# Attention and gated projections on one core: the opening's loads, buffers and casts put in another order

## The chip, the core and the metric

The kernel runs on one core of one Trainium2 chip. The metric is the device time of one execution in microseconds (us). Each execution also records the span of the core and the mean clock that was granted to TensorE, as a share of full speed.

## The reference, cut to what matters

Four batches, 8 heads, 768 positions, head size 64. Blocks of 32 positions attend to their neighbours, to the first and last block and to three drawn blocks. The result is normalised per row and goes through a gated projection of 512 to 1536 and back.

```python
scores = scale * np.matmul(q, k.transpose(0, 1, 3, 2))
scores = np.where(mask, scores, -1e9)              # block mask, 24 x 24 blocks
attn = softmax(scores)
x = np.matmul(attn, v)                             # -> (3072, 512), heads side by side
xn = x / np.sqrt(np.mean(x * x, -1) + 1e-6) * rms_g
g, val = xn @ w_gate, xn @ w_val                   # 512 x 1536 each
out = (g * sigmoid(g) * val) @ w_out               # 1536 x 512
```

## The kernel before

Everything is fed to TensorE. Keys and queries of a pair of heads are cast to bf16 (`aug`), transposed (`XA`), multiplied to scores, exponentiated by ScalarE into a probability buffer (`pt`), and multiplied with the cast values (`vaug`). The mask is part of the product: 24 extra columns of `aug` carry it. For batch 0 the transposes of keys and queries are done by TensorE; for later batches they are DMA transposes (`XA<-aug`), issued on SyncE. The normalised rows (`xq`) must be transposed too (`xn`): for the first NPET units by TensorE, later by a DMA transpose (`xn<-xq`), also issued on SyncE. A unit is a set of query rows: units 0 to 2 are 128 rows each, unit 3 is 384 rows, all of batch 0; units 4 to 9 are 384 rows each of batches 1 to 3. A small scheduler in the program sorts all operations by modelled times at build time; each engine then runs its list in order.

```python
# loads of batch 0; pairs of heads g = 0..3; i = 0 keys, 1 queries, 2 values; 384 KB a keys or values tile
load0(0, 0, slice(0, 1)); load0(0, 0, slice(1, 2))
load0(0, 1, x=slice(0, D)); load0(0, 1, x=slice(D, HD))
load0(1, 0); load0(0, 2); load0(1, 1)              # all on SyncE's queue
# ... later, by the scheduler:
for g, i in ((2, 0), (2, 1), (1, 2), (3, 0), (3, 1), (2, 2), (3, 2)): ...
# the mask columns of both aug buffers, by ScalarE
for t in aug:
    nc.scalar.copy(out=t[:, 1, :, :, D:KQ], in_=qm.unsqueeze(1).to_broadcast([P, 2, NC, NB]))
# zeros behind the mask columns, wanted before batch 1's DMA transposes
def zero_pad():
    for t in aug:
        nc.gpsimd.memset(t[:, :, :, :, KQ:P], 0.0)
# probability buffers, transposed-row buffers, units whose rows TensorE transposes
NPT, NXN, NHP, NPET = 3, 3, 2, 4
# rows of unit u, transposed by the DMA when u >= NPET
op(("cp", u), {"DMA": 1.8}, [("xq", u, t) for t in range(nt)], (-2, u), lambda e, p, u=u: xt(u), ...)
```

The softmax here doesn't subtract the row's maximum and nothing guards it: scores larger than these inputs give would overflow.

Of the kernel before, what the change touches and what calls it, by code (L numbers as in the profile page):

```python
# [9 lines left out]
FP32 = mybir.dt.float32  # L10
# [3 lines left out]
ALU = mybir.AluOpType  # L14
# [3 lines left out]
def kernel(  # L18
# [27 lines left out]
    AHEAD, HURRY, HURU = 0.8, ("av", "xo", "sq", "rsq", "xq", "tr", "cp"), 0  # L46
    NSTARV = 3
    AH = {"uu": 0.3, "hp": 0.3}
# [41 lines left out]
    A = [raw.tile([P, 3, 2, NC * D], FP32, name="qkv", tag="qkv") for g in range(3)]  # L90
    def load0(g, i, e=slice(0, 2), x=None):
        x = x or slice(0, HD if i == 1 else NC * D)
        nc.sync.dma_start(
            out=A[g][:, i, e, x], in_=(kv, qv, vv)[i][0, :, 2 * g:2 * g + 2][:, e, x])

    load0(0, 0, slice(0, 1))
    load0(0, 0, slice(1, 2))
    load0(0, 1, x=slice(0, D))
    load0(0, 1, x=slice(D, HD))
    load0(1, 0)  # L100
    load0(0, 2)
    load0(1, 1)
# [84 lines left out]

    for t in aug:
        nc.scalar.copy(out=t[:, 1, :, :, D:KQ], in_=qm.unsqueeze(1).to_broadcast([P, 2, NC, NB]))  # L189

# [38 lines left out]
    def gate_pool(g):  # L229
        nc.gpsimd.tensor_copy(out=scf, in_=A[g][:, 1, 0, 0:1])  # L230

# [14 lines left out]

    def zero_pad():
        for t in aug:
            nc.gpsimd.memset(t[:, :, :, :, KQ:P], 0.0)

# [29 lines left out]
    def exp(u, pr, g):  # L280
        b, c0, nt = UNITS[u]
        kt, w = KT[nt], nt * P
        if (u, pr) not in pts:
            if nt == 1:
                t_ = work.tile([P, 2, NC, 2, w], BF16, name="pt", tag="pt", bufs=NPT)
                pts[u, pr // 2 * 2], pts[u, pr // 2 * 2 + 1] = t_[:, 0], t_[:, 1]
            else:
                pts[u, pr] = work.tile([P, NC, 2, w], BF16, name="pt", tag="pt", bufs=NPT)
        s_ = tiles.pop(("s", u, pr, g))
        nc.scalar.activation(  # L290
            out=pts[u, pr][:, g * kt:(g + 1) * kt].rearrange("p j e w -> p e j w"),
            in_=s_[:, :, 0:kt * w].rearrange("p e (j w) -> p e j w", w=w),
            func=AF.Exp, scale=SCALE)
# [26 lines left out]
    def sq(u, t):  # L320
        nt = UNITS[u][2]
        if u not in mss:
            mss[u] = work.tile([P, nt], FP32, name="ms", tag="ms")
        sc = work.tile([P, DM], BF16, name="sc", tag="sc", bufs=1)
        x = xos[u][:, t].rearrange("p h d -> p (h d)")
        nc.vector.tensor_tensor_reduce(  # L326
            out=sc, in0=x, in1=x, scale=1.0 / DM, scalar=1e-6, op0=ALU.mult, op1=ALU.add,
            accum_out=mss[u][:, t:t + 1])

    def rsq(u):  # L330
        nt = UNITS[u][2]
        r = work.tile([P, nt], FP32, name="rs", tag="rs")
        nc.gpsimd.tensor_tensor(out=r, in0=mss[u], in1=nhalf[:, 0:nt], op=ALU.pow)  # L333
        mss[u] = r
# [97 lines left out]

    NPT, NXN, NHP, NPET = 3, 3, 2, 4
    pools = {n: [0.0] * c for n, c in (
# [6 lines left out]
    banks = [0.0] * 8  # L441
    banks[2] = 5.9
    S_, S3, TP1 = [(0, 1), (2, 3)], [(0, 1), (2, 3), (4, 5)], [(6,), (5,), (4,)]
    held = {}
    LAT = {"PE": 0.2, "ACT": 0.16, "DVE": 0.08, "POOL": 0.1, "DMA": 1.9}
    ops, end, made = [], {}, {}
# [16 lines left out]

    def load3(e, p):
        A.append(raw.tile([P, 3, 2, NC * D], FP32, name="qkv", tag="qkv"))
        load0(3, 0)

    ld0(("l", 0, 0), 1.2)
    ld0(("l", 0, 1, 0), 0.2)
    ld0(("l", 0, 1, 1), 0.35)  # L470
    ld0(("l", 1, 0), 1.0)
    ld0(("l", 0, 2), 1.1)
    ld0(("l", 1, 1), 0.6)
    for g, i in ((2, 0), (2, 1), (1, 2), (3, 0), (3, 1), (2, 2), (3, 2)):
        ld0(("l", g, i), 0.6 if i == 1 else 1.1,
            load3 if (g, i) == (3, 0) else lambda e, p, g=g, i=i: load0(g, i),
            [], [("raw", 3)] if (g, i) == (3, 0) else [])
    ld0(("lg",), 0.7, lambda e, p: nc.sync.dma_start(
# [6 lines left out]
    for i in range(NWC + NOC):  # L485
        for m in range(2 if i < NWC else 1):
            def wi(e, p, i=i, m=m):
                if i + m == 0:
                    gate_pool(3)
                load_w(i, m) if i < NWC else load_wo(i - NWC)  # L490
            op(("wi", i, m), {"POOL": 0.9 + 0.2 * (i + m == 0)},
               [prev] if prev else [("l", 3, 0)], (2, i, m), wi)
            if (i, m) in ((2, 0), (3, 0)):
                made["wi", i, m]["deps"] += [("rsq", i - 2)]
            prev = ("wi", i, m)
        if i == 0:
            ld0(("q2",), 2.2, q2_, [], [("hp", ("q2",))])
            op(("w0",), {"DMA": 2.1}, [("wi", 0, 0)], (0,), None)
            seq.append(("w0",))
        op(("w", i), {"DMA": 4.2 if i else 2.1}, [prev], (0,), None)  # L500
        seq.append(("w", i))
        if i >= NWC - 1:
            seq += [("ld", NP + i - NWC + 1, j) for j in range(3)]
# [3 lines left out]
    KP = {True: [((0,), 0, 3), ((1,), 0, 3), ((0, 1), 3, 6)], False: [((0,), 0, 6), ((1,), 0, 6)]}  # L507
    QP = {True: [((0, 1), 0, 1), ((0, 1), 1, 3), ((0, 1), 3, 6)], False: [((0, 1), 0, 3), ((0, 1), 3, 6)]}
    for g in range(NP):
        a_ = g % NAUG  # L510
        rr = [("raw", g)]
        if g:
            op(("fk", g), {"DVE": 0.57, "POOL": 0.84}, [("l", g, 0)], (-1, g, 0),
               lambda e, p, g=g: fillk(g, e), [(f"aK{a_}", g)], rr)
        for n_, (es, lo, hi) in enumerate(QP[g == 0]):
            dep = ("q2",) if lo == 3 else ("l", 0, 1, n_) if g == 0 else ("l", g, 1)
            pri = (-1, g, 1) if lo == 0 else (2.5, g, lo)
            fe = {"DVE": 0.09 + 0.085 * (hi - lo), "POOL": 0.1 + 0.13 * (hi - lo)}
            op(("fq", g, lo), {"ACT": 0.2} if g == 0 and lo == 0 else fe, [dep], pri,
               lambda e, p, a=(g, lo, hi): fillq(*a, e), [(f"a{'QR'[lo == 3]}{a_}", (g, lo == 3))],  # L520
               rr if lo < 3 else [("hp", ("q2",))])
        for i in range(2):
            for n_, (es, lo, hi) in enumerate((KP, QP)[i][g == 0]):
# [3 lines left out]
                else:  # L527
# [4 lines left out]
                   pri, lambda e, p, a=(g, i, es, lo, hi): tpx(*a, p),  # L532
                   [(TP1[:1] if i and lo == 3 else TP1, key), (f"X{g}", g)],
                   [(res, g)] if i == 0 else [(res, (g, lo == 3))])
                de = {"DVE": 0.07 + m_ * P / 1560.0}
                ac = {"ACT": 0.15 + m_ * P / 1200.0}
                if g == 0 and i == 0:
                    de = (de, ac, {**de, **ac})[n_]
                elif i and lo == 3 or g == 0 and lo == 0:
                    de.update(ac)  # L540
# [8 lines left out]
    pools["aK0"] = []  # L549
    op(("zp",), {"POOL": 1.8}, [], (9,), lambda e, p: zero_pad(), at=24.0)  # L550
    for g in range(NP, B * NP):
        b, pr = divmod(g, NP)
        gate = {NP: 2, NP + 1: 3, NP + 2: 4, NP + 3: 5}.get(g)
        for i in range(3):
# [6 lines left out]
            if i < 2:  # L561
                op(("fill", g, i), {"DVE": 0.57}, [("ld", g, i), ("zp",)] + [
                    ("tp", g_, i_, 0, 3 * i_) for g_ in (2, 3) for i_ in range(2)],
# [17 lines left out]
    for u, (b, c0, nt) in enumerate(UNITS):  # L581
        w, last = nt * P, c0 + nt == NC
        ng = NC // KT[nt]
        for pr in range(NP):
            g0 = b * NP + pr
            pk = pr // 2 if nt == 1 else pr
            for g in range(ng):
                op(("qk", u, pr, g), {"PE": 2 * KT[nt] * mm(w)}, dep0(g0, b, c0, nt, KT[nt], g),
                   (2 if u else 0.5, u, pr, g), lambda e, p, a=(u, pr, g): qk(*a, p),
                   [(S3 if u < NOPEN else S_, ("s", u, pr, g)), ("pt", (u, pk))],  # L590
                   [(f"X{g0 % NSLOT}", g0)] if last and g == ng - 1 else [])
# [6 lines left out]
               lambda e, p, a=(u, pr): av(*a, p), [([(7,)] + [(6,)] * (u < 3), ("o", u, pr)), ("xo", u)],  # L598
               ([("pt", (u, pk))] if nt > 1 or pr % 2 else []) + ([(f"va{b % 2}", b)] if last and pr == NP - 1 else []))
            op(("xo", u, pr), {"DVE": 0.4 + w / 960.0}, [("av", u, pr)], (0, u, pr),  # L600
               lambda e, p, a=(u, pr): xo(*a), [], [(None, ("o", u, pr))])
        for t in range(nt):
            op(("sq", u, t), {"DVE": 0.75}, [("xo", u, pr) for pr in range(NP)], (1, u, t),
               lambda e, p, a=(u, t): sq(*a))
        op(("rsq", u), {"POOL": 0.9}, [("sq", u, t) for t in range(nt)], (0, u), lambda e, p, u=u: rsq(u))
        for t in range(nt):
# [13 lines left out]
        for f in range(NF // fg):  # L620
            n_ = fg * w
            op(("g", u, f), {"PE": fg * NP * mm(w)}, [("cp", u), ("w", w_of[f])], (4, u, f, 1),
               lambda e, p, a=(u, f): proj(*a, wg, "gp", p), [([(4,)], ("g", u, f)), ("hp", HG[u])])
            op(("th", u, f), {"ACT": 0.12 + n_ / 1200.0}, [("g", u, f)], (2, u, f),
# [22 lines left out]

    free = {"PE": 5.0, "ACT": 5.4, "DVE": 4.8, "POOL": 4.5, "DMA": 2.1}
    left = {o["key"]: len(o["deps"]) for o in ops}
# [39 lines left out]
    while ready:  # L689
# [27 lines left out]
        for names, key, nme in got:  # L717
# [11 lines left out]
        end[o["key"]] = fin + (  # L729
            3.7 if o["key"] == ("q2",) else 8.0 if o["key"][0] == "ld" and o["key"][1] >= NP else 4.0 if o["key"][0] == "turn"  # L730
            else LAT[e])
# [54 lines left out]
```

## Time and profile before

| what | kernel before |
|---|---|
| time, median of the first three executions | 312.75 us (312.03 to 312.91) |
| time, all 34 executions measured beside the experiments | 310.98 to 317.55 us |
| span of the profiled execution | 310.0 us (time 311.69 us) |
| TensorE busy | 97% |
| end of TensorE's last matmul in the trace | 306.24 us |

The prediction below shows the page's head, the stage table and the opening's timeline (start, busy us, engine, line, operation, how many, and in brackets the idle time ahead with what ended it). Two more views of the kernel before matter for what follows. First, of TensorE's waits (who waits at which line for whom: us in total, times, longest us), the one for rows that the DMA transposes:

```profile
PE PS L378 <- DMA xn<-xq: 0.6, 1, 0.6
```

These are unit 4's rows, the first that the DMA transposes in this kernel.

### The profile page before, as it was taken

What the parts mean: (1) busy time and instruction counts of PE and PEld (TensorE: products, weight loads), DVE (VectorE), ACT (ScalarE), POOL (GpSimd) and SP (SyncE); (2) the same over time, 40 slices, a digit from 0 to 9 for tenths busy, and PEclk for the clock granted to TensorE, in tenths of its full rate; (3) what the DMA queues carried; (4) which work ended last, traced back from release to release, by engine and by line L of the source; (5) the groups of instructions that cost most, each with busy time, mean ns of one, the idle gap of its engine ahead of it and who ended that gap; (6) DMA issues with size and microseconds to landing.
All of it is one profiled execution on the core that took longest, in us unless ns stands there. A gap on an engine that the chain in (4) does not pass through costs nothing.

```text
span 310.0 us, 7365 instructions
## 1 busy us (share of the span) xinstructions
PE 300.3 (97%) x3033; PEld 199.6 (64%) x3063; DVE 191.0 (62%) x423; ACT 207.0 (67%) x325; POOL 24.6 (8%) x42
## 2 busy tenths in 40 slices
PE   8899999999999999999999999999999999999995
PEld 7798888766666556666666666666665546556543
DVE  5769656785658978757754844664489607727500
ACT  5898988688877887878777787878743133323221
POOL 3457100010000001001000100010001000000000
PEclk9999999999999999999999999999999999999998
DMA  7999999999999999931893030021000041010022
GB/s 220 312 238 184 195 268 207 211 331 269 225 296 207 248 209 324 241 111 36 165 159 73 31 87 2 34 42 45 2 34 3 19 128 40 0 68 2 0 105 102
DMA packets 70661, 42.42 MB, mean 137 GB/s; under 512 B 48356, under 2 KB 67556, under 8 KB 70628
## 3 DMA queue, kind: packets, MB, share of 16 engines
q1 hardware_dynamic: 64800, 37.23, 48.1%
q0 software_dynamic: 5792, 4.72, 9.8%
q8 instruction: 24, 0.39, 0.5%
q14 instruction: 9, 0.07, 0.1%
q10 hardware_dynamic: 36, 0.00, 0.0%
HBM read 28.57 MB, written 6.29 MB: 112 GB/s over the span
## 4 chain that ended last, share of the span: by engine, by line
PE 90%; ACT 3%; DMA 3%; issue 1%; DVE 1%; SPq 0%; ACTq 0%; DVEq 0%
PE PS L378 40%; PE PS L417 19%; PE PS L275 18%; PE PS L304 11%; ACT pt L290 2%; DMA qkv<-in_q_dram 2%; DMA xn<-xq 1%; PE PS L129 1%; PE PS L257 1%; ACT XA L109 0%; PE PS L351 0%; ACT th L387 0%; DVE uu L393 0%; PE PS L154 0%; ACT aug L189 0%
## 5 line engine op out<-in xcount | busy, mean ns | idle before, releaser
L290 ACT ACTIVATE pt<-PS 128x768 bf16<-128x768 f32 x192 | 145.4, 812 | 35.4 <-PE PS L275 33.9
L393 DVE SCALAR_TENSOR_TENSOR uu<-th,PS 128x384 bf16<-128x384 bf16 x96 | 53.1, 554 | 62.0 <-ACT th L387 59.8
L275 PE MATMUL PS<-XA 88*128 88x384 bf16 (+1 forms) x480 | 81.2, 293 | 0.8 <-ACT pt L290 0.6
L378 PE MATMUL PS<-xn,wg 128*128 128x384 bf16 (+1 forms) x480 | 75.4, 294 | 0.9 <-DMA xn<-xq 0.6
L378 PE MATMUL PS<-xn,wv 128*128 128x384 bf16 (+1 forms) x480 | 75.5, 293 | 0.0
L387 ACT ACTIVATE th<-PS 128x384 bf16<-128x384 f32 x96 | 47.4, 493 | 33.5 <-PE PS L378 31.1
L417 PE MATMUL PS<-wo,hp 128*128 128x512 bf16 (+1 forms) x270 | 65.8, 369 | 1.6
L404 DVE TENSOR_TENSOR hp<-uu,PS 128x384 bf16<-128x384 bf16 x96 | 51.4, 551 | 14.8 <-PE PS L378 13.8
L378 PEld LDWEIGHTS <-wg 128*128 128x128 bf16 x480 | 41.6, 97 | 24.6 <-issue 1.5
L378 PEld LDWEIGHTS <-wv 128*128 128x128 bf16 x480 | 41.5, 97 | 23.3 <-issue 0.2
L275 PEld LDWEIGHTS <-XA 88*128 88x128 bf16 x480 | 39.4, 97 | 21.7 <-issue 1.8
L417 PEld LDWEIGHTS <-hp 128*128 128x128 bf16 x300 | 29.0, 98 | 26.9
L304 PEld LDWEIGHTS <-pt 128*128 128x128 bf16 x1152 | 41.2, 97 | 6.0 <-issue 0.7
L304 PE MATMUL PS<-vaug,pt 128*128 128x65 bf16 x1152 | 42.7, 193 | 0.6 <-DVE xo L316 0.6
L427 ACT ACTIVATE yo<-PS 128x512 f32<-128x512 f32 (+1 forms) x23 | 13.3, 579 | 28.0 <-PE PS L417 27.1
L333 POOL TENSOR_TENSOR rs<-ms,nhalf 128x3 f32<-128x3 f32 (+1 forms) x10 | 7.9, 787 | 199.7 <-DVE ms L326 199.7
L316 DVE TENSOR_TENSOR xo<-PS,rz 128x384 f32<-128x384 f32 (+1 forms) x40 | 19.1, 477 | 1.4
L340 DVE SCALAR_TENSOR_TENSOR xq<-xo,rs,gB 128x512 bf16<-128x512 f32 x24 | 17.5, 754 | 0.2 <-POOL rs L333 0.2
L326 DVE CUSTOM_DVE_ANT_0 sc<-xo 128x512 bf16<-128x512 f32 x24 | 16.5, 688 | 0.3
L113 DVE CAST aug<-qkv 128x768 bf16<-128x768 f32 (+2 forms) x30 | 15.2, 524 | 2.3 <-DMA qkv<-in_k_dram 1.8
L315 DVE RECIPROCAL rz<-PS 128x6 f32<-128x6 f32 (+1 forms) x40 | 7.4, 184 | 14.8 <-PE PS L304 14.6
L113 DVE CAST vaug<-qkv 128x768 bf16<-128x768 f32 x14 | 7.8, 554 | 1.9 <-DMA qkv<-in_v_dram 1.9
(54 smaller groups left out, 69.0 us busy)
## 6 DMA issues: line engine op xcount, KB each, us to landing
qkv<-in_v_dram SPq DMA_DIRECT2D x16, 384.0 KB, 5.9
out_dram<-yo SPq DMA_DIRECT2D x23, 256.0 KB, 2.0
qkv<-in_k_dram SPq DMA_DIRECT2D x15, 384.0 KB, 4.9
qkv<-in_q_dram SPq DMA_DIRECT2D x12, 384.0 KB, 5.1
wg<-in_moe_w_gate_dram POOLq DMA_DIRECT2D x4, 384.0 KB, 8.1
wv<-in_moe_w_val_dram POOLq DMA_DIRECT2D x4, 384.0 KB, 9.2
wo<-in_moe_w_out_dram POOLq DMA_DIRECT2D x2, 768.0 KB, 16.6
q<-in_q_dram SPq DMA_DIRECT2D x1, 768.0 KB
```

What stands on the lines that cost most here:

```text
L113: nc.vector.tensor_copy(out=out, in_=in_)
L275: nc.tensor.matmul(out=s_[:, e, j * w:(j + 1) * w], lhsT=x[0:KQ, 0, e, jt * P:(jt + 1) * P], rhs=x[0:KQ, 1, e, c0 * P:c0 * P + w], start=T ...
L290: nc.scalar.activation(out=pts[u, pr][:, g * kt:(g + 1) * kt].rearrange("p j e w -> p e j w"), in_=s_[:, :, 0:kt * w].rearrange("p e (j w) ...
L304: nc.tensor.matmul(out=o_[:, t, e, :], lhsT=pt[:, jt, e, t * P:(t + 1) * P], rhs=va[:, (2 * pr + e) * NC + jt, 0:D + 1], start=(jt == 0), ...
L316: nc.vector.tensor_tensor(out=xos[u][:, :, 2 * pr:2 * pr + 2, :], in0=o_[:, :, :, 0:D], in1=rz.unsqueeze(3).to_broadcast([P, nt, 2, D]), o ...
L326: nc.vector.tensor_tensor_reduce(out=sc, in0=x, in1=x, scale=1.0 / DM, scalar=1e-6, op0=ALU.mult, op1=ALU.add, accum_out=mss[u][:, t:t + 1])
L340: nc.vector.scalar_tensor_tensor(out=xqs[u][:, t, :], in0=xos[u][:, t].rearrange("p h d -> p (h d)"), scalar=mss[u][:, t:t + 1], in1=gB, o ...
L378: nc.tensor.matmul(out=p_[:, j, :].rearrange("p (t w) -> p t w", w=P), lhsT=w_[:, c, f_ * P:(f_ + 1) * P], rhs=xns[u][:, :, c, :], start=( ...
L387: nc.scalar.activation(out=t_, in_=tiles["gp", u, f], func=AF.Tanh, scale=0.5)
L393: nc.vector.scalar_tensor_tensor(out=t_, in0=tiles.pop(("th", u, f)), scalar=1.0, in1=tiles.pop(("gp", u, f)), op0=ALU.add, op1=ALU.mult)
L404: nc.vector.tensor_tensor(out=hps[u][:, f * fg:(f + 1) * fg, :], in0=tiles.pop(("uu", u, f)), in1=tiles.pop(("vp", u, f)), op=ALU.mult)
L417: nc.tensor.matmul(out=tiles["yp", u, t, h], lhsT=hps[u][:, f, t * P:(t + 1) * P], rhs=wo[:, f, x], start=(f == 0), stop=(f == NF - 1))
```

## The change

The intent is to start TensorE's useful work sooner. The keys and queries of all four pairs are loaded ahead of any values. A fourth room for raw tiles is borrowed from the output weights, which come later. One exponential group more can run ahead in a borrowed buffer (`ph`). The first query tile comes on ScalarE's queue and is cast by GpSimd, and GpSimd makes the second mask copy. The zero fill goes from GpSimd to VectorE, and later. The square sum of a 128-row unit is split in two. Unit 3's rows are transposed by the DMA instead of TensorE (NPET 3). The diff, cut:

```diff
-    load0(0, 1, x=slice(0, D))
+    load0(0, 1, x=slice(0, D), eng=nc.scalar)
     load0(0, 1, x=slice(D, HD))
     load0(1, 0)
-    load0(0, 2)
     load0(1, 1)
...
-    for t in aug:
-        nc.scalar.copy(out=t[:, 1, :, :, D:KQ], in_=qm...)
+    nc.scalar.copy(out=aug[0][:, 1, :, :, D:KQ], in_=qm...)      # aug[1] by GpSimd
...
-            nc.gpsimd.memset(t[:, :, :, :, KQ:P], 0.0)
+        nc.vector.memset(aug[i][:, :, :, :, KQ:P], 0.0)
...
+                if u == 0 and pr == 2:
+                    t_ = work.tile([P, NF, 3 * P], BF16, name="ph", tag="hp", bufs=NHP)
...
-    NPT, NXN, NHP, NPET = 3, 3, 2, 4
+    NPT, NXN, NHP, NPET = 3, 3, 2, 3
...
-        A.append(raw.tile([P, 3, 2, NC * D], FP32, name="qkv", tag="qkv"))
+    A.append(wo.rearrange("p f x -> p (f x)")[:, 0:12 * NC * D].bitcast(FP32)...)
...
-    for g, i in ((2, 0), (2, 1), (1, 2), (3, 0), (3, 1), (2, 2), (3, 2)):
+    for g, i in ((2, 0), (2, 1), (3, 0), (3, 1), (0, 2), (1, 2), (2, 2), (3, 2)):
...
-                elif i and lo == 3 or g == 0 and lo == 0:
+                elif g == 0 and lo == 0:
                     de.update(ac)          # ScalarE may make the copy, too
```

(Cut: the split square sum, the scheduler's start times and latencies, and which bank a group may take.)

## The prediction

Its sum comes to 1.7 + 1.0 + 0.66 - 0.6, rounded to 2.8 us, and 312.75 less that to the 309.9 predicted. "Its 128x384 cast" is GpSimd's. That the two memsets (24.62 to 26.39) made the cast at 24.03 as long as 2.57 us, which the term of 1.0 us counts on, was the reading of one trace; the cause was not shown. The 260 GB/s is the estimate: the first three slices of the profile of before have 220, 312 and 238 GB/s, its stage table 279 for 4.66 to 25.29 us.

> **What bounds the kernel now.** I read the page first, to see which engine is full, then the time table by stage, then the waits of TensorE, then the order of work in the opening.
>
> ```profile
> span 310.0 us, 7365 instructions
> PE 300.3 (97%) x3033; PEld 199.6 (64%) x3063; DVE 191.0 (62%) x423; ACT 207.0 (67%) x325; POOL 24.6 (8%) x42
> ...
> PE 90%; ACT 3%; DMA 3%; issue 1%; DVE 1%; SPq 0%; ACTq 0%; DVEq 0%
> ```
>
> TensorE is busy for 97% of the span and makes up 90% of the chain that ended last. No other engine passes 67%. So the end moves only if TensorE gets less work or starts its useful work earlier.
>
> 97% hides two things: filler matmuls on a zero tile count as busy, and so do modelled pipeline ends. So I count useful work by start-to-start times. In the timeline 12 projection matmuls of 128 columns take 0.67 us (56 ns each), two of 384 columns 0.33 us (163 ns), 36 of probabilities times values 1.14 us (32 ns), three of 512 columns 0.65 us (217 ns), 6 transposes 0.34 us. With the program's counts: scores 144 x 0.056 + 336 x 0.163 = 62.9; probabilities times values 1152 x 0.032 = 36.6; gate and value projections 288 x 0.056 + 672 x 0.163 = 125.7; output 276 x 0.217 + 24 x 0.11 = 62.5; transposes of keys and queries 96 x 0.057 = 5.5; of the normalised rows 24 x 0.055 = 1.3. Sum: 294.5 us. The first useful transpose starts at 4.66, the last matmul ends at about 306.2. So some 7 us are lost on TensorE between those points. The head (4.7) and the tail (3.8) come on top. These 7 us are all that the change can win by better order. The stage table shows where they lie:
>
> ```profile
> 4.66:25.29 20.63, 19.00 (x353) 17.75 (x352) 14.54 (x38) 18.36 (x29) 11.14 (x17) 1.00 1.07 279
> 25.29:34.34 9.05, 8.19 (x136) 7.05 (x132) 7.21 (x21) 7.95 (x14) 5.38 (x8) 1.00 1.20 180
> 34.34:60.00 25.66, 25.55 (x403) 21.35 (x405) 15.93 (x34) 20.08 (x33) 0.00 (x0) 1.00 1.17 219
> ```
>
> (Stretch, length, then busy us of TensorE, weight loads, VectorE, ScalarE, GpSimd, then clock, DMA share, GB/s.) 25.29 is the first projection matmul. Useful work before it: 138 score matmuls (7.8), 108 with values (3.4), 84 + 4 transposes (5.0), together 16.2 of 20.6 us: 4.4 lost. From there to 34.34: 7.7 of 9.05, so 1.3 lost. From 34.34 on TensorE is full. Until the first projection, ScalarE paces: an exponential of 128x768 starts every 0.73 us, and its matmuls fill less than that. The lines that carry it:
>
> ```profile
> 5.22 0.31 ACT L109 CAST aug<-qkv 128x128 bf16<-128x128 f32 x1
> 6.88 4.33 ACT L290 ACTIVATE pt<-PS 128x768 bf16<-128x768 f32 x6 [0.58 <-PE PS L275]
> 10.31 0.56 DVE L113 CAST aug<-qkv 128x768 bf16<-128x768 f32 x1 [1.66 <-DMA qkv<-in_k_dram]
> 12.38 4.57 ACT L290 ACTIVATE pt<-PS 128x768 bf16<-128x768 f32 x6 [1.17 <-PE PS L275]
> 17.31 2.92 ACT L290 ACTIVATE pt<-PS 128x768 bf16<-128x768 f32 x4 [0.35 <-PE PS L275]
> 23.68 0.79 ACT L109 COPY XA<-PS 88x768 bf16<-88x768 bf16 x1
> 24.03 2.57 DVE L113 CAST aug<-q 128x384 bf16<-128x384 f32 x1
> 24.62 1.76 POOL L249 MEMSET aug<- 128x960 bf16 x2
> 25.25 0.69 PEld L378 LDWEIGHTS <-wg 128*128 128x128 bf16 x12
> ```
>
> ScalarE rounds the first query tile (5.22), begins exponentials at 6.88, starves 1.17 us at 12.38 because keys of pair 2 came at 10.31 behind the values of pairs 0 and 1, starves 0.35 at 17.31, and spends 0.79 on a transposed query tile at 23.68.
>
> [...] an issue on SyncE takes 0.47 us, and the DMA share is already 1.07 in the opening[...]. [...] the cast at 24.03 took 2.57 us beside the two memsets on GpSimd, where the other casts of this shape took about 0.35. [...] here its 128x384 cast takes 0.50 us against 0.35 on VectorE, so it is slower but usable off the path.
>
> **The change part by part.** I compared the instruction orders of both builds.
>
> *First exponential.* Out of ScalarE's queue go one of two mask copies (0.35), the cast (0.31) and one copy of transposed keys (0.48). The new chain: mask copy 4.64 to 5.04; 12 key transposes on TensorE 4.66 to 5.34, two query ones to 5.46; 0.2 to hand over; copy of 88x256 0.37 to 6.03; scores at 6.08; the exponential 0.48 later, as it is now (6.40 to 6.88): 6.56. The query tile lands at about 1.4 + 2.9 = 4.3, and GpSimd's cast (estimate 0.3) is done by 4.7. Gain 0.3.
>
> *Keys and queries first.* One 384 KB value tile less ahead of keys 2 (1.45 us at the 260 GB/s of that stretch), two less ahead of keys 3. Keys 2 arrive near 8.9 in place of 10.3, keys 3 near 11 in place of 12.9. Exponential 11, the first of pair 2, is due at 6.56 + 10 x 0.73 = 13.9. So the 1.17 goes. Values 0 come at about 12.2 and 1 at 13.5, and are first needed to free a probability buffer for exponential 17 (18.2), because the extra buffer raises the room from 12 to 16 exponentials: the 0.35 goes too. Keys 3 lie in room of the output weights, which are loaded later, so the raw-buffer wait (2.4 us on SyncE) goes.
>
> *First projection.* 22 exponentials instead of 21 now stand before the copy of the normalised rows: 6.56 + 22 x 0.73 = 22.6. But the rms chain may be later: second query half lands at 20.5, GpSimd makes two casts (1.0), then the power (0.57): 22.1; multiply 0.75, transposes and hand-over 0.4, copy 0.59: first projection at about 23.9, against 25.29. The order holds one more score group (0.34) ahead of it, and the same 108 and 84 others. Gain 1.4 + 0.3 = 1.7.
>
> *25 to 35 us.* The memsets leave GpSimd, which frees VectorE from the 2.57 cast and TensorE from the 0.6 wait it caused at 27.05; three query copies (2.4 us of ScalarE) go to VectorE. Of 1.3 lost I give back 1.0. Memsets on VectorE and the split square sum (0.25 in place of 0.7 on the path) are small.
>
> *Transposes of unit 3* move to the DMA: 12 x 0.055 = 0.66 us of TensorE work gone.
>
> *Against it.* Weights are loaded at the DMA's pace, one 384 KB chunk per 2 us (landings 22.7, 24.6, 26.6, 28.5 ...), and this does not move. The second gate group needs the chunk at 26.6, its place in the new order is about 26.7; the second half of the output weights lands at 50.7, while its first use would come near 50.2. I take 0.6 for such waits.
>
> Sum: 1.7 + 1.0 + 0.66 - 0.6 = 2.8 us. 312.75 - 2.8 = 309.95, rounded to 309.9.
>
> **Rivals.** (1) The weights' transfers become the bound: everything before is then hidden, and only the 0.66 and about 1 us remain: 311. For it: the cadence of 2 us and a DMA share of 1.07 to 1.20; against it: the old order had 2 to 3 us of slack at most of these points. (2) GpSimd becomes the late one: it gets eleven casts instead of eight, and the power stands behind two casts; if each drags, the first projection stays near 25 and the time near 312. (3) The opening is won in full, with no new wait: 4.4 becomes about 2 and 1.3 becomes nothing; with the 0.66, 308.3. (4) A new DMA wait for the transposed rows of unit 3 or for batch 1, whose first transpose was issued at 45.5: 0.5 to 1 us back.
>
> **Range and chances.** Rivals 3 and 1 give 308 to 311, single runs scatter by 0.5: 307.8 to 312.0. Faster by over 2% means under 306.5, which needs 6.3 us, nearly all of the 7 lost plus the 0.66: 0.03. Slower by over 2% would need a new stall of 9 us: 0.02.
>
> **What would show it.** Right: first exponential near 6.6, no ScalarE gap of 1 us before the 22nd, first projection near 23.9, 12 transposes of normalised rows, VectorE casts near 0.35. Wrong: TensorE waiting on weights for over 1 us, on GpSimd's casts, or on the DMA's transposed rows near 65; or the opening shortened while TensorE idles as much between 40 and 110 us.

## More of the kernel before

In the timeline (start, busy us, engine, line, operation, how many, and in brackets the idle time ahead with what ended it):

```profile
104.90 2.29 SPq L366 DMA_TRANSPOSE xn<-xq  x1
109.14 0.81 PE L378 MATMUL PS<-xn,wg 128*128 128x384 bf16 x4 [0.57 <-DMA xn<-xq]
```

A DMA transpose issued at 104.90 is awaited until 109.14.

## The result, and the profile after

| | before | after |
|---|---|---|
| median us of the four executions | 312.83 (312.03 to 313.71) | 309.23 (309.0 to 309.68) |
| ratio, 95% interval | | 0.9886 (0.9857 to 0.9915) |
| span of the profiled execution | 310.0 | 307.4 |
| TensorE's last matmul ends | 306.24 | 303.62 |

A ratio is the mean time of one kernel's fast runs over that of the other's of the same rounds, so not quite the ratio of the medians. Executions over 1.5% slower than the fastest of the same kernel are left out of the means. The change makes the kernel 1.1% faster; the traces differ by 2.6 us, less than the medians, because the profiled execution of the kernel before (311.69) was faster than all four in the table.

The page's head, and the row of the chain of work that ended last:

```profile
span 307.4 us, 7325 instructions
PE 299.2 (97%) x3022; PEld 199.6 (65%) x3050; DVE 192.1 (62%) x434; ACT 202.4 (66%) x317; POOL 25.1 (8%) x44
...
PE 95%; ACT 2%; DMA 2%; issue 1%; DVE 0%; ACTq 0%
```

TensorE's share of the chain went from 90% to 95%: it remains the bound, with less in between. The stage table of the kernel after (same columns and stretches as in the prediction):

```profile
4.66:25.29 20.63, 20.22 (x371) 19.68 (x371) 15.77 (x46) 18.35 (x27) 12.30 (x20) 1.00 1.14 289
25.29:34.34 9.05, 8.70 (x153) 7.50 (x152) 7.80 (x24) 8.06 (x13) 4.28 (x6) 1.00 1.28 194
34.34:60.00 25.66, 25.50 (x391) 21.37 (x391) 18.10 (x40) 18.25 (x30) 0.86 (x1) 1.00 1.14 234
60.00:110.00 50.00, 48.58 (x488) 30.84 (x491) 35.22 (x73) 40.29 (x61) 0.85 (x1) 1.00 1.05 265
```

TensorE's busy time in the first stretch is 1.2 us higher, in the second 0.5 higher. Busy time counts the ends of matmuls, so I also counted useful work, as the prediction did: every matmul that isn't a filler at its start-to-start time at full clock (56 ns for 128 columns, 163 for 384, as in the prediction), and the loss is the time since 4.66 less that work. Before: 4.5 us lost at 25.29, 5.9 at 34.34, 6.6 at 60. After: 3.3, 3.9, 4.6. Some records of matmuls are missing from a trace, so such a count is good to some 0.5 us.

The opening's timeline, to be set beside the prediction's:

```profile
4.72 1.77 PE L254 MATMUL PS<-ident,aug 128*88 128x128 bf16 x14
7.17 4.43 ACT L292 ACTIVATE pt<-PS 128x768 bf16<-128x768 f32 x6 [0.98 <-PE PS L272]
8.85 0.56 DVE L112 CAST aug<-qkv 128x768 bf16<-128x768 f32 x1
10.53 1.28 POOL L110 CAST aug<-wo 128x768 bf16<-128x768 f32 x2 [0.57 <-DMA wo<-in_k_dram]
11.98 2.92 ACT L292 ACTIVATE pt<-PS 128x768 bf16<-128x768 f32 x4 [0.38 <-PE PS L272]
18.75 0.95 POOL L110 CAST aug<-q 128x384 bf16<-128x384 f32 x2 [0.41 <-DMA q<-in_q_dram]
23.56 0.59 ACT L365 COPY xn<-PS 128x512 bf16<-128x512 bf16 x1
24.39 0.69 PEld L384 LDWEIGHTS <-wg 128*128 128x128 bf16 x12
```

Keys of pair 2 are cast at 8.85 where it was 10.31, keys of pair 3 at 10.53. ScalarE's gap of 1.17 us has become 0.38, and the gap of 0.35 at 17.31 is gone. But the first exponential starts at 7.17, later than before (6.88). The first projection starts at 24.39 in place of 25.25.

The part that nothing in the opening tells is the new wait. The longest of TensorE's waits, then the timeline around it:

```profile
PE PS L384 <- DMA xn<-xq: 1.2, 1, 1.2
```

```profile
60.94 2.07 DVE L346 SCALAR_TENSOR_TENSOR xq<-xo,rs,gB 128x512 bf16<-128x512 f32 x3
64.20 0.36 SPq L437 DMA_DIRECT2D out_dram<-yo  x1
64.65 2.58 SPq L372 DMA_TRANSPOSE xn<-xq  x1
69.40 0.81 PE L384 MATMUL PS<-xn,wg 128*128 128x384 bf16 x4 [1.16 <-DMA xn<-xq]
```

Unit 3's rows are written at 63.0 (60.94 plus 2.07). Their transpose is issued at 64.65, behind an output store, and TensorE stands 1.16 us for it, until 69.40. The last of six loads issued ahead of it on the same queue landed at 67.17.

### The profile page after: what moved, and what is told of

It is laid out like the page before. It is cut to its first block, busy times and chain, and to the rows that moved or that the text cites. A ratio compares the mean times of both kernels' runs of the same rounds, so it can differ in the third digit from the quotient of the medians.

```text
span 307.4 us, 7325 instructions
## 1 busy us (share of the span) xinstructions
PE 299.2 (97%) x3022; PEld 199.6 (65%) x3050; DVE 192.1 (62%) x434; ACT 202.4 (66%) x317; POOL 25.1 (8%) x44
## 4 chain that ended last, share of the span: by engine, by line
PE 95%; ACT 2%; DMA 2%; issue 1%; DVE 0%; ACTq 0%
PE PS L384 41%; PE PS L272 19%; PE PS L423 19%; PE PS L306 12%; PE PS L254 2%; DMA xn<-xq 2%; ACT pt L292 1%; PE PS L128 1%; PE PS L153 0%; PE PS L357 0%; ACT yo L433 0%; PE PS L183 0%; DVE zt L115 0%; ACTq L433 0%
## 5 line engine op out<-in xcount | busy, mean ns | idle before, releaser
L292 ACT ACTIVATE pt<-PS 128x768 bf16<-128x768 f32 x188 | 142.9, 812 | 33.7 <-PE PS L272 33.2
L384 PEld LDWEIGHTS <-wg 128*128 128x128 bf16 x480 | 41.4, 98 | 23.9 <-issue 1.6
L306 PEld LDWEIGHTS <-pt 128*128 128x128 bf16 x1128 | 40.5, 97 | 5.7
L331 DVE CUSTOM_DVE_ANT_0 sc<-xo 128x512 bf16<-128x512 f32 (+1 forms) x24 | 16.3, 680 | 0.2
L112 DVE CAST aug<-qkv 128x768 bf16<-128x768 f32 (+1 forms) x28 | 14.5, 538 | 0.1
L112 DVE COPY XA<-PS 88x768 bf16<-88x768 bf16 (+2 forms) x17 | 8.5, 518 | 2.7 <-PE PS L254 2.7
```

The costliest lines, as they stand in the source:

```text
L112: nc.vector.tensor_copy(out=out, in_=in_)
L292: nc.scalar.activation(out=pts[u, pr][:, g * kt:(g + 1) * kt].rearrange("p j e w -> p e j w"), in_=s_[:, :, 0:kt * w].rearrange("p e (j w) ...
L306: nc.tensor.matmul(out=o_[:, t, e, :], lhsT=pt[:, jt, e, t * P:(t + 1) * P], rhs=va[:, (2 * pr + e) * NC + jt, 0:D + 1], start=(jt == 0), ...
L331: nc.vector.tensor_tensor_reduce(out=sc[:, z], in0=x, in1=x, scale=1.0 / DM, scalar=mss[u][:, 0:1] if nt == 1 and t else 1e-6, op0=ALU.mul ...
L384: nc.tensor.matmul(out=p_[:, j, :].rearrange("p (t w) -> p t w", w=P), lhsT=w_[:, c, f_ * P:(f_ + 1) * P], rhs=xns[u][:, :, c, :], start=( ...
```

## The experiments

Times are medians of six executions, with the range, beside the kernel before on the same chip. The medians of the kernel before were 311.97, 312.55, 312.61 and 312.19 us. All outputs are right.

### The changed kernel again

No edit. The question was whether the late first exponential belongs to the change or to TensorE's clock.

> The changed kernel, unaltered, a second time. Two things are read from it. First the anchor for the other runs: 309.2 us, 3.6 us under the kernel before. Second the TensorE clock in the opening: in the profile of the changed kernel the key transposes from 4.72 us on started 107 ns apart and went to 56 ns only at about 7.0 us, in that of the kernel before they were at 56 ns from 4.6 us on. Theory P (the phase of the clock's warm-up is chance): in this run the step falls elsewhere, anywhere from 4.5 to 8 us, and where it falls before 5 us the first exponential starts near 6.6 us as predicted, not at 7.17. Rival C (the change itself delays the warm-up, by the ScalarE queue or GpSimd work): the step is at 7.0 us again and the first exponential at 7.2.

Measured: 309.35 us (308.82 to 310.65), ratio 0.9906 (0.9870 to 0.9941). The first exponential started at 6.45. The same 14 transposes took less time:

```profile
4.66 1.27 PE L254 MATMUL PS<-ident,aug 128*88 128x128 bf16 x14
```

In this execution TensorE's clock went to full speed at 4.52 us, in the profile after at 7.09. Ten profiles taken here have the changed kernel's work up to the first exponential, and its start follows the clock step: step at 4.52 and 4.85, exponential at 6.45 and 6.45; 5.75 and 5.91, 6.77 and 6.77; 6.26, 6.81; 6.78, 7.07; 6.83, 7.09; 6.99, 7.16; 7.09, 7.17; 7.25, 7.17. In the profile of the kernel before the step came at 4.56. So the change did move the first exponential from 6.88 to 6.45, and the 7.17 is chance. The traces show one thing more of these steps: each stretch between two of them is a whole number of times the shortest, 3.41 us (303.79 us in the profile of before is 89 times that, 300.37 in the profile after 88 times, 6.83 us twice).

That the exponentials begin sooner does not yet bring the rest forward. In this profile ScalarE then stood idle twice at once:

```profile
7.95 0.81 ACT L292 ACTIVATE pt<-PS 128x768 bf16<-128x768 f32 x1 [0.68 <-PE PS L272]
...
9.10 2.92 ACT L292 ACTIVATE pt<-PS 128x768 bf16<-128x768 f32 x4 [0.35 <-PE PS L272]
```

The next query columns were cast by GpSimd only at 6.59, when their load was in, and TensorE waited 0.62 us for that. ScalarE's 22 exponentials ended at 23.84 here and at 23.42 in the profile after, where they had begun 0.72 us later.

This profile also shows that the wait for unit 3's rows isn't a fixed 1.2 us:

```profile
71.02 0.81 PE L384 MATMUL PS<-xn,wg 128*128 128x384 bf16 x4 [1.86 <-DMA xn<-xq]
```

### The old load order

```diff
     load0(1, 0)
+    load0(0, 2)
     load0(1, 1)
-    for g, i in ((2, 0), (2, 1), (3, 0), (3, 1), (0, 2), (1, 2), (2, 2), (3, 2)):
+    for g, i in ((2, 0), (2, 1), (1, 2), (3, 0), (3, 1), (2, 2), (3, 2)):
```

> The changed kernel with the loads of batch 0 in the old order (values of pair 0 third, values of pair 1 ahead of keys of pair 3), all else kept, the room in the output weights too. Theory O (keys and queries first is what keeps ScalarE fed): keys of pair 2 come near 10.2 us again, ScalarE idles about 0.5 to 1.2 us before its exponential of pair 2 or 1 near 11 to 13 us, and the run is 0.5 to 1.5 us slower than the changed kernel. Rival M (the room for pair 3 and the extra buffer did it, the order only follows): within 0.3 us.

Measured: 313.21 us (311.62 to 315.69), ratio 1.0028 (0.9985 to 1.0072), 3.9 us above the changed kernel: the direction was right and the size more than twice what was expected. The gaps on ScalarE came back:

```profile
9.93 2.92 ACT L293 ACTIVATE pt<-PS 128x768 bf16<-128x768 f32 x4 [1.34 <-PE PS L273]
...
13.49 3.62 ACT L293 ACTIVATE pt<-PS 128x768 bf16<-128x768 f32 x5 [0.65 <-PE PS L273]
```

The loss was 6.2 us at 34.34 (after: 3.9, second profile 4.8). Some 1.4 us of the 3.9 is therefore the opening. The rest isn't explained: there was a wait of 1.5 us for unit 3's rows, but that is no longer than in the changed kernel (1.16 and 1.86), and the two profiles differ by only 1.9 us at TensorE's last matmul. Two of the six executions had a mean clock under 0.996. With the old load order nothing is left of the change's gain.

### The new load order alone

The kernel before, with keys and queries ahead of values and pair 3's raw tile in the room of the output weights, and nothing else of the change.

```diff
     load0(1, 0)
-    load0(0, 2)
     load0(1, 1)
-        A.append(raw.tile([P, 3, 2, NC * D], FP32, name="qkv", tag="qkv"))
+    A.append(wo.rearrange("p f x -> p (f x)")[:, 0:12 * NC * D].bitcast(FP32)...)
-    for g, i in ((2, 0), (2, 1), (1, 2), (3, 0), (3, 1), (2, 2), (3, 2)):
+    for g, i in ((2, 0), (2, 1), (3, 0), (3, 1), (0, 2), (1, 2), (2, 2), (3, 2)):
```

> The kernel before with one part of the change alone: keys and queries of all pairs ahead of values, and pair 3's raw data in the room of the output weights. Buffers, engines and the rest as before. Theory O2 (order and extra probability buffer only work together: with room for 12 exponentials the late values stop the 13th): ScalarE has no gap of 1.17 us near 12 us, but one of 0.5 to 2 us near 16 to 18 us, and the time is within 0.7 us of the kernel before, 312 us. Rival A (the order alone makes most of the gain): 1.5 to 3 us faster, 309 to 310.5 us.

Measured: 310.67 us (310.05 to 311.17), ratio 0.9918 (0.9886 to 0.9949); 1.9 us under the kernel before by medians, 2.6 by means. The exponentials run without a gap once they have begun, though they begin late:

```profile
7.50 12.24 ACT L289 ACTIVATE pt<-PS 128x768 bf16<-128x768 f32 x17 [1.18 <-PE PS L274]
```

The loss was 4.6 us at 34.34, that is 1.3 less than before. So the load order alone (with the room that it needs) is the larger part of the gain.

### The first query tile as before

The tile again on SyncE's queue and cast by ScalarE, both mask copies again on ScalarE.

```diff
-    load0(0, 1, x=slice(0, D), eng=nc.scalar)
+    load0(0, 1, x=slice(0, D))
-    nc.scalar.copy(out=aug[0][:, 1, :, :, D:KQ], in_=qm...)
+    for t in aug:
+        nc.scalar.copy(out=t[:, 1, :, :, D:KQ], in_=qm...)
```

> The changed kernel with the first query tile on SyncE's queue again and rounded by ScalarE, which also makes both mask copies; all else kept. Theory Q0 (it shortens the way to the first exponential by one cast and one mask copy on ScalarE): with TensorE's clock at full from 4.6 us the first exponential starts near 6.9 us in place of 6.45, and the kernel is 0.2 to 0.6 us slower than the changed one. Rival D (the data of the next pairs set the pace from the third exponential on, so the start is worth nothing): within 0.2 us.

Measured: 310.7 us (310.12 to 315.09), ratio 0.9929 (0.9886 to 0.9972). The median of the five fast ones is 310.52. Against the variant that keeps the changed opening (309.1, with the zero fill on GpSimd, below) that is 1.4 us slower, more than expected, but the intervals of the two ratios overlap. The first exponential started at 7.47, with the clock step at 6.25; with the step at 6.26 the changed opening had it at 6.81. So this part is worth 0.66 us at the first exponential. That any of the 1.4 us comes from it isn't shown: the loss at 34.34 us was 4.6 in this run and 4.4 in the other, too close to tell apart. As far as they go, the profiles speak for rival D, that the data of the next pairs set the pace.

### Without the extra probability buffer

```diff
-                if u == 0 and pr == 2:
+                if False:
-            ptn = ("hp", "ph") if u == 0 and pk == 1 else ("pt", (u, pk))
+            ptn = ("pt", (u, pk))
```

> The changed kernel without the extra probability buffer: unit 0's heads 4 to 7 take one of the three ordinary buffers. Theory B (room for 16 exponentials instead of 12 is needed because values come late): the 13th exponential must wait for values 0 and 1 (landing 12.0 and 13.1 us) and their products, so ScalarE idles 0.5 to 2 us between 13 and 20 us and the run is 0.4 to 1.5 us slower than the changed kernel. Rival N (values land early enough for 12 buffers): within 0.2 us.

Measured: 315.12 us (314.55 to 316.62), ratio 1.0090 (1.0052 to 1.0127), 5.8 us above the changed kernel. Expected was 0.4 to 1.5. The gap on ScalarE that theory B expected is there, 0.67 us at 17.01 us (0.67 again, at 17.62, in the other kernel without the buffer, further below). But the opening isn't where the time went: the loss at 34.34 was 5.0 us, against 4.8 in the changed kernel's second profile. It went here:

```profile
64.22 0.44 SPq L80 DMA_DIRECT2D qkv<-in_k_dram  x1
64.76 4.65 SPq L372 DMA_TRANSPOSE xn<-xq  x1
72.57 1.46 PE L384 MATMUL PS<-xn,wg 128*128 128x384 bf16 x4 [3.40 <-DMA xn<-xq]
```

The scheduler, given one buffer less, sorted the list anew, and one more load of 384 KB came ahead of unit 3's transpose. TensorE waited 3.40 us, and then its four matmuls took 1.46 us where they take 0.81. The stage table of this run says why (the third number from the end is the clock, 1.00 in the ten us before):

```profile
70.00:80.00 10.00, 7.43 (x59) 4.69 (x60) 2.77 (x6) 2.74 (x5) 0.00 (x0) 0.66 1.06 251
```

The clock was at half from 71.11 to 77.94 us, 6.83 us. It fell while TensorE stood idle (since 69.17); 1.46 us of the stretch were waiting anyhow, so the half speed cost some 2.7 us more, beside the 3.40. All six executions had a mean clock of 0.987 to 0.993, and no execution of the unaltered changed kernel was under 0.997. So the run doesn't tell what the buffer is worth; it tells what a wait of this kind costs.

### Unit 3's rows by TensorE, as before the change

```diff
-    NPT, NXN, NHP, NPET = 3, 3, 2, 3
+    NPT, NXN, NHP, NPET = 3, 3, 2, 4
```

> The changed kernel with the normalised rows of unit 3 transposed on TensorE again (12 transposes, 0.66 us of work). Theory W: moving them to the DMA saved 0.66 us of TensorE and put a wait of 1.16 us in its place (the first gate group of unit 3 at 69.4 us waits for them), so this kernel is 0.3 to 0.6 us faster than the changed one, and the wait near 69 us is gone. Rival S: the wait only moves (unit 3's copy then takes 1.4 us of ScalarE, which delays exponentials, and a wait of 0.6 us at unit 4 comes back as in the kernel before), so it is 0.0 to 0.7 us slower.

Measured: 310.61 us (309.59 to 310.85), ratio 0.9937 (0.9899 to 0.9974), 1.3 us slower than the changed kernel by medians (the intervals of the ratios overlap). The wait near 69 us was gone and one of 1.1 us for unit 4's rows had come, near 105. So the 12 transposes (0.66 us) were paid for nothing: the wait moved on.

### Unit 3's rows hurried

The square sum, the power and the scaling of unit 3 get the scheduler's early start that unit 0 has.

```diff
-                ahead = AHEAD if k_[0] in HURRY and k_[1] <= HURU and (
+                ahead = AHEAD if k_[0] in HURRY and (k_[1] <= HURU or k_[1] == 3) and (
```

> The changed kernel, with the squares, the power and the scaling of unit 3's rows put ahead of other VectorE work in the list (the order that units 0 has already), so that SyncE can issue unit 3's transposes some microseconds earlier. Theory Q (the wait of 1.2 to 1.9 us near 69 us comes from the transposes being issued late, 64.65 us, with loads and an output ahead of them in SyncE's order, while TensorE has filler left): the wait is gone and the kernel is 1.0 to 2.0 us faster than the changed kernel, about 307.8 us. Rival V (VectorE work taken out of turn holds up gate and value groups, or the wait only moves to unit 4): no more than 0.3 us faster.

Measured: 315.44 us (311.89 to 316.27), ratio 1.0051 (1.0003 to 1.0099). The wait near 69 us did go, and the loss from 65 to 80 us was 0.2 us (after: 1.8). But from 34.34 to 60 us the loss was 1.8 us (after: 0.7), which speaks for the first part of rival V. And unit 4 paid, its second part, again with the clock at half for 6.83 us, from 107.25 on:

```profile
108.41 1.44 PE L384 MATMUL PS<-xn,wg 128*128 128x384 bf16 x4 [3.45 <-DMA xn<-xq]
```

The one execution with a clock of 1.0 took 311.89, the others, at 0.987 to 0.995, took 313.67 to 316.27.

### The zero fill back on GpSimd

```diff
-        nc.vector.memset(aug[i][:, :, :, :, KQ:P], 0.0)
+        nc.gpsimd.memset(aug[i][:, :, :, :, KQ:P], 0.0)
-        op(("zp", i), {"DVE": 0.4}, ..., at=ZPAT)
+        op(("zp", i), {"POOL": 0.9}, ..., at=24.0)
```

> The changed kernel with the two clearing memsets back on GpSimd at the old place in the list. Theory L [...]: some VectorE instruction with SBUF operands near 25 to 35 us takes over 1.5 us in place of its usual 0.35 to 0.75, and the kernel is 0.3 to 1.0 us slower. Rival E (in the new order VectorE has no such cast at that time: the query halves are cast by GpSimd itself): no long VectorE instruction, but the weights' issues on GpSimd move up to 1.8 us later; within 0.3 us.

Measured: 309.1 us (308.75 to 311.36), ratio 0.9879 (0.9842 to 0.9916): not slower than the changed kernel at all. The two fills ran at 25.12 and 26.67 and no VectorE cast was long beside them. The cast of 2.57 us in the kernel before was real, but the changed order has no such cast next to the fills any more. This part of the change is worth nothing measurable.

### Output stores on another queue

```diff
-        nc.sync.dma_start(out=dst[:, c0 + t, h * n:(h + 1) * n], in_=o)
+        q_ = nc.gpsimd if u < 3 else nc.sync
+        q_.dma_start(out=dst[:, c0 + t, h * n:(h + 1) * n], in_=o)
```

> The changed kernel with one edit: the output stores of units 0 to 2 are issued on GpSimd's queue, so that SyncE no longer stands at one of them (issued at 64.2 us, though the normalised rows of unit 3 were written at 63.0) before it issues the DMA transpose of those rows at 64.65. All engine orders else stay. Theory S (the gain of the opening is partly paid back in TensorE's wait for those rows, 1.2 and 1.9 us in two profiles, because the transpose is issued late): the transpose is issued near 63.1 to 63.5, the wait near 69 falls under 0.5 us, the time is 308.0 to 308.8, some 1 us under the changed kernel's 309.3. Rival: the transposes are slow because the queue's engines are busy with the 384 KB loads ahead of them, so an earlier issue only lengthens them: the wait stays at 1 us or more, the time at 309.0 to 309.7.

Measured: 309.55 us (308.78 to 312.06), ratio 0.9892 (0.9848 to 0.9937): the same as the changed kernel. The transpose was issued 1.1 us sooner, and TensorE waited no less (1.74 us, against 1.16 and 1.86):

```profile
63.56 2.35 SPq L372 DMA_TRANSPOSE xn<-xq  x1
70.39 0.81 PE L384 MATMUL PS<-xn,wg 128*128 128x384 bf16 x4 [1.74 <-DMA xn<-xq]
```

Almost 7 us from the issue to the use. So the issue alone isn't what is late. The rival holds: of the six loads of 384 KB issued before it the last landed only at 67.83, and the rows came 2.56 us after that. In the two profiles of the unaltered kernel it was the same: rows 2.23 us after the last load's landing in one (67.17), 2.17 us in the other (68.85).

### Three loads behind the rows

The keys, queries and values of pair 7 wait until unit 3's transpose has been issued; all else is left to the scheduler.

```diff
-            op(("ld", g, i), {"DMA": 1.1}, [("w", gate)] if gate is not None and i == 0 else [],
+            op(("ld", g, i), {"DMA": 1.1}, ([("w", gate)] if gate is not None and i == 0 else []) + [("cp", 3)] * (g == NP + 3),
```

> The changed kernel with one more dependency: the three loads of keys, queries and values of pair 7 (384 KB each, issued at 59.6, 60.05 and 60.56 us, the last landing at 67.17) wait until the transposes of unit 3's normalised rows have been issued. The earlier run with output stores on GpSimd's queue showed that an earlier issue alone does not help: issued at 63.56 in place of 64.65, the rows still came at 70.3. Theory B (the rows' transposes run only after the loads queued ahead of them; what counts is the backlog, not the issue): issued near 63 with only the three loads of pair 6 ahead, the rows land near 66, the wait of 1.2 to 1.9 us near 69 is gone (under 0.3), and the loss counted from 65 to 70 us stays under 0.5 where it was 1.3 to 2.0. The time is then 308.0 to 309.0, unless pair 7, which now comes about 5 us later, makes TensorE wait for its own transposes: rival G, a wait of 1 us or more for XA after 70 us and 309.5 to 311.5. Rival T (the transposes are slow by themselves, about 5 to 7 us from issue): the wait near 69 stays at 1 us or more.

Measured: 313.1 us (311.51 to 314.67), ratio 1.0007 (0.9951 to 1.0063). Two places of the timeline, the first near unit 3, the second near unit 4:

```profile
63.26 1.47 SPq L372 DMA_TRANSPOSE xn<-xq  x1
...
67.61 0.81 PE L384 MATMUL PS<-xn,wg 128*128 128x384 bf16 x4 [0.17 <-DMA xn<-xq]
...
115.95 0.97 PE L384 MATMUL PS<-xn,wg 128*128 128x384 bf16 x4 [2.64 <-DMA xn<-xq]
117.35 1.49 PE L384 MATMUL PS<-xn,wv 128*128 128x384 bf16 x4
```

Only three loads stood ahead, and they had landed at 63.19, before the issue. The rows came 4.35 us after the issue (66 had been expected, so the transpose by itself is slower than I took it), the wait was 0.17, and the loss was 4.2 us at 65 and 4.6 at 80, the least of all profiles here. So two things make the rows late in the changed kernel, the backlog of loads and the late issue. The backlog alone is enough, as the run before showed. The late issue alone makes little or some wait, by an estimate: 64.65 and 4.35 make 69.0, and TensorE stood ready at 68.2. With the median of 3.7 us from issue to landing that the profile of before lists for its own transposes of rows, it would be 68.35, hardly a wait. From issue to use it was 4.35 us with no load outstanding at the issue, 4.75, 5.46 and 6.83 with loads under way (the profile after, the second profile, the run before this one). But the time isn't better. The scheduler put the loads elsewhere, unit 4's rows came 2.64 us too late, and the clock fell to half for 3.41 us (the 1.49 above). None of the theories expected this; it wasn't XA that was late.

### Two units more by TensorE, with and without the extra buffer

Units 3 and 4 by TensorE; the second kernel has the two edits of the run without the extra probability buffer besides.

```diff
-    NPT, NXN, NHP, NPET = 3, 3, 2, 3
+    NPT, NXN, NHP, NPET = 3, 3, 2, 5
```

> The changed kernel with the rows of units 3 and 4 transposed by TensorE (NPET 5 in place of 3): 24 transposes more, 24 x 0.055 = 1.3 us of work, and no DMA wait for rows before unit 5. The scheduler rearranges what follows. Theory S: both fragile waits (near 69 and near 108) are gone, so the time is the changed kernel's less 1.2 to 1.9 plus 1.3: 308.8 to 309.6, and without executions that run to 311. Rival M (the wait simply moves on to unit 5, as it moved to unit 4 with NPET 4): a wait of over 1 us for transposed rows after 115 us and a time of 310.0 to 311.0.

> As a_npet5, but without the extra probability buffer; against a_npet5 it shows what that buffer is worth when no unit before the fifth waits for DMA-transposed rows. Theory S (of the 5.8 us that the buffer's removal cost, nearly all was the 3.4 us wait near 69 and the half clock after it): 0.3 to 1.2 us slower than a_npet5, 309.3 to 310.8, and the clock stays full. Rival: the buffer itself carries the gain through the opening: 3 us or more slower than a_npet5, over 312.

Measured: with the buffer 309.97 us (309.06 to 310.38), ratio 0.9894 (0.9862 to 0.9927); without it 310.06 (309.6 to 310.55), ratio 0.9898 (0.9863 to 0.9932). The profiles of both show no wait of 0.2 us or more for transposed rows anywhere. The first of them from 60 to 110:

```profile
60.00:110.00 50.00, 49.54 (x514) 32.32 (x519) 36.66 (x75) 40.05 (x59) 1.04 (x1) 1.00 1.02 265
```

TensorE stands idle 1.0 us less here than in the kernel after, whose wait of 1.16 us is gone, and has 24 transposes more to do (1.3 us by the prediction's figure). So for the time it comes to much the same: the waits avoided are about the work added, and the 309.97 lies 0.4 above what was expected. What it does change is the scatter: none of these twelve executions was over 310.55 or under a clock of 0.998. And it gives the clean comparison that the earlier run without the buffer couldn't: where no early unit waits for the DMA, the extra probability buffer is worth 0.1 us, within the scatter. In the opening alone the two profiles differ more: at 34.34 us the kernel with the buffer had lost 4.5 us, the one without 5.4. One profile of each doesn't settle whether that is the buffer.

No version was clearly faster than the changed kernel: 309.1 with the fills on GpSimd, 309.23 and 309.35 unaltered, 309.55 and 309.97 are not told apart by these runs.

## Why the prediction was right or wrong

The time, 309.2 to 309.4 against 309.9 predicted, is in the range, and the gain stays under 2%. By its steps (two slips of arithmetic change nothing: 384 KB at 260 GB/s take 1.5 us, not 1.45, and the unrounded sum 2.76 makes 309.99):

**First exponential, 6.88 to 6.56.** The step was right, and rather too small: 6.45 when the clock is up in time, as it was in the profile of before. The prediction left out that the time of the clock's step (4.52 to 7.25 us) moves this point by up to 0.7 us (6.45 to 7.17) from one execution to the next. It compared one profile of before, in which the clock rose early, with an order worked out for the same clock. It also carried the start on, at 0.73 us each, to a 22nd exponential that ends at 22.6. It ended at 23.42 in the profile after, and at 23.84 in the second, which had begun 0.72 us sooner. So the earlier start did not reach the first projection: with the first exponential at 6.45 it came at 25.33 and 24.57, with it at 7.17 at 24.42 and 24.59.

**Keys and queries first.** Right on the loads: keys 2 at 8.85 (said 8.9), keys 3 at 10.53 (said 11). On the gaps right in part: in the first profile the 1.17 shrank to 0.38 (it was to go) and the 0.35 is gone; in the second, whose clock rose as early as before's, ScalarE still stood idle 0.68, 0.35 and 0.38 us, 1.4 in all against before's 1.5. The old load order, put back, brought the gaps back and took the whole gain; the new order alone gave 1.9 of it. But the part of it credited to the extra probability buffer is confirmed only as far as the gap: without the buffer a gap of 0.67 us came back near 17 us, and yet, with the later waits out of the way, the time is the same.

**First projection, 23.9, a gain of 1.7.** It came at 24.4, and in the other profiles of the same opening between 24.6 and 25.3; the loss counted at 25.29 fell by 1.2 in the first profile and by 0.3 to 1.1 in the others. The chain to the normalised rows was right in its times and wrong in its reason. GpSimd's power ended at 21.97 (said 22.1), but not because it stood behind the second query half and its casts: that half was in use at 18.75, not at 20.5, the two casts were done by 19.7, and GpSimd then stood idle 1.70 us until VectorE's square sum was there. The agreement of the two times is luck. In the first profile ScalarE went from its exponentials into the copy of the rows with 0.14 us between, so both chains met there; in five of the seven others the copy waited 0.3 to 0.9 us for the transposes.

**25 to 35 us, 1.0.** Loss in that stretch fell from 1.4 to about 0.6: some 0.8 gained. Its reasons failed. Putting the fills back on GpSimd cost nothing. And the run with the new load order alone, which still has the fills on GpSimd and the three query copies on ScalarE (21.33, 28.81 and 30.47), lost only 0.5 us in the same stretch, with no long cast in it; the run with the old load order, which keeps both moves, lost 1.3. So the gain came with the order of the loads, and neither of the two moves made it. The reading of the long cast was too sure as well: it began at 24.03 and the first memset at 24.62, when a cast of 0.35 us would have been over. From 23.89 to 24.64 GpSimd was issuing a load of weights. No run tells the two apart.

**Unit 3's transposes, 0.66.** The work is gone, but the sum booked it as gain and named the wait only as a rival. The rival came true, mostly above its 0.5 to 1 us: 1.16 and 1.86 us in two profiles of the unaltered kernel, 0.7 to 1.7 in three of the experiments that keep this part. A wait there of over 1 us was on the prediction's own list of signs of being wrong. With TensorE doing the transposes for two more units, which adds 1.3 us of work, the time was the same within the scatter.

**Waits on weights, 0.6 against.** This failed. "This does not move" was wrong: the first gate weights landed at 20.49 in place of 22.67, though they were issued no sooner (14.00, before 13.82), and no wait on weights showed. With the new load order and its room alone it was 20.41, with the old order in that room 21.32. So the room seems to be the larger part: SyncE no longer waits 2.4 us for a raw buffer, and the opening's loads are through sooner; that reason is argued. In its place stood the wait for the transposed rows.

**The sum.** By 34.34 us the eight profiles that share the changed opening show 3.9 to 4.8 us lost (mean 4.3) against 5.9 in the one profile of before: some 1.6 gained, where the prediction had 2.7 less the waits. Of its rivals the first did not come, and the second only in part: the longest wait of TensorE for a cast by GpSimd was 0.62 us, in the second profile. Later come 0.66 saved, 1.2 to 1.9 lost near 69, and before's own wait of 0.57 near 109, gone. Worked out for each profile by its own losses, these terms make 2.1 us for the first and 0.5 for the second. At TensorE's last matmul the traces differ by 2.6 and 1.15 us, so some 0.6 us lies in what the terms leave out, about the error of the count; the medians differ by 2.6 to 3.6. The one profile of before was among the faster executions, and a part of the difference in means is the clock: 9 of 34 executions of before had a mean clock under 0.996, and these took 313.8 us or more (one of them is left out of the ratios); of ten executions of the changed kernel none had. That these nine had a long wait for unit 4's rows is likely from what the experiments show, but they weren't profiled, and it stays open.

So the predicted time was right in part by luck. The gain of the opening was put too high by about 1 us; the loss on weights did not come, and a larger wait of another kind stood in its place; by the steps the gain should have fallen short. What made up for it was in good part the kernel before: the prediction counted its gain on a profile of 311.69 us and took it off a median of 312.75, and the executions that were slower than that profile lost time that the prediction did not look for.

## What to carry to other kernels

When a DMA transpose takes over work from a full engine, count what is queued ahead of it, not only its own duration: here the rows came 4.35 us after the issue with no load outstanding and, with loads still under way, 4.2 to 7.8 us after it, the more the later those landed. A wait of TensorE that looks harmless at 1 us has a step in its price: at 2.64 us and more it took the clock with it here, for 3.4 to 6.8 us at half speed, which added some 1.7 to 2.8 us to the wait (the list below says what of a wait counts). And where a build-time scheduler sorts the work anew, removing one part changes the order far away; an experiment with such a part needs its stages looked at before its total is believed, as the run without the extra buffer shows.

## What the traces show of the clock and of transposes

- After an idle of TensorE of 2.64 us (three loads behind the rows) the clock was at half for 3.41 us, with idles of 3.40 and 3.45 us (without the extra buffer; unit 3's rows hurried) for 6.83 us, and idles of 1.74 and 1.86 us (output stores on another queue; the changed kernel again) did not halve it. In the two longest cases the clock fell before the idle was over, 1.94 us (71.11 after 69.17) and 2.29 us (107.25 after 104.96) into it. What fits all 14 traces is the idle within one stretch of 3.41 us, the trace being cut so that the clock's steps fall on the cuts. The clock fell 17 times (14 of them after the last matmuls); the stretch just before had 1.94 us of idle or more each time (1.94, 2.10, 2.14, 2.17, 2.29, 2.64 and up). No stretch that left the clock up had more than 1.88 (the next are 1.79 and 1.74), the ends of matmuls being modelled. So in these traces the limit lay between 1.88 and 1.94 us; that a wait of 2 to 3 us can cross it or not, as it falls on the cuts, is an estimate from this count.
- Over 14 profiles with the same filler matmuls at the start the clock's step to full speed came between 4.52 and 7.25 us, a spread of 2.7 us, which, in the ten with the changed opening, moved the first exponential between 6.45 and 7.17. In the profile after, where it came at 7.09, transposes of 128 columns started 107 ns apart before it and 56 ns after it.
- A group of 18 transposes by TensorE (128x88 each) was busy for 1.17 us in several profiles of the changed opening, which is at most 65 ns each, and within a group they start 56 ns apart: the pace of full speed. Whether transposes alone would keep the clock up, no run here shows.
- A DMA transpose of rows took 4.35 us from issue to use with no load outstanding. Behind loads queued by the same issuing engine and still under way it was 4.2 us (the kernel before, at 104.90) to 7.8 us from the issue, in three profiles 2.2 to 2.6 us after the landing of the last load ahead.
